# A gated mix of Fourier mixing and sliding-window attention: four engines in listed order, row sums inverted as 128 x 16, and earlier loads

## The chip, the cores and the metric

The kernel runs on one core of one Trainium2 chip. The metric is device time in microseconds (us) of one execution, lower is better. A core has a matrix engine (PE, TensorE), a vector engine (DVE, VectorE), an activation engine (ACT, ScalarE), a general engine (POOL, GpSimd) and a queue that issues data transfers (SP, SyncE). ACT can issue transfers too. Each of them works through its own list of instructions in the order of that list, and waits at an instruction until what it needs is there. "The order" below is the order of these lists.

## The reference

There are 2048 rows of 512 numbers, x. One branch is a Fourier mixing layer, the other an attention layer with 32 heads of 16 columns in which each row sees itself and the 255 rows before it. A gate per row mixes them.

```python
a = einsum("bsd,ed->bse", x, dft_hid_re); b = einsum("bsd,ed->bse", x, dft_hid_im)
y = einsum("ts,bse->bte", dft_seq_re, a) - einsum("ts,bse->bte", dft_seq_im, b)
q, k, v = (x @ wqkv).reshape(B, S, 3, 32, 16).transpose(2, 0, 3, 1, 4)
scores = einsum("bhqd,bhkd->bhqk", q, k) * 16 ** -0.5      # kept where 0 <= q - k < 256
o = einsum("bhqk,bhkd->bhqd", softmax(scores), v) @ wo     # heads joined
g = sigmoid((x * gate_w).sum(-1))
return g * y + (1 - g) * o
```

## The kernel before

**The dense part** is everything that is an ordinary matrix product: the projections of x to q and k (`dqk`, four groups of heads times four quarters of 512 rows), to v (`dv`, 16 blocks of 128 rows), to the two hidden Fourier products (`dab`), and the two sequence products with the 2048 x 2048 cosine and sine matrices (`dc`). It is written as a Python generator, `dense()`, which yields after every matmul, so that the attention loop can draw from it a few matmuls at a time. Each operand is split into a rounded part `hi` and a rest `lo`, and a product is three matmuls. While attention runs, a matmul is done as two halves of 64 rows of the contraction (L248, "64*128 64x512"), the upper half some time behind the lower one; a copy of one number by ACT (`token`, L267) stands between them. What follows a finished block (`then`, `late`) is listed when its upper half has been listed.

**The attention part** walks through 128 units n (8 sets of four heads times 16 blocks of 128 rows) with two pairs of heads p each. A step (n, p) lists, on PE, two score matmuls `s` (L396) on which DVE takes a masked row minimum of the negated scores (L400, written to `ml`), then dense matmuls (`fill`), then, 11 units later (`LAG`), the transposed scores `t` (L455), of which ACT takes the exponent (L458) into `pt` and POOL cuts the corners (L461, L465), then dense matmuls again. `FILL_PAIR` / 4 dense matmuls go into each `fill`; there are four per unit. `s` and `t` share four banks of PSUM, so an `s` may start only when DVE has read the one that had its bank. Every four units (one group u, 32 groups in all) the minima are turned with PE (L414), stored and loaded back as rows of the operand `ring` (`ml_split`, `ml_turn`, `ml_rows`, `m_ring`).

Every four units `visit` multiplies `pt` with v into one PSUM bank `o` (L482). v has a column of ones, so row 16 of every 32 rows of `o` holds the sums of the softmax. `o_take` (L495) then copies `o` with ACT into an `ev` buffer (L501), takes the reciprocal of the whole 128 x 512 bank with DVE into a second one (L502), and stores the four rows that matter to `l_scr` in DRAM with four transfers from SP. `o_load` (L507) loads each of them back to 32 partitions, and `o_out` (L512) multiplies (L516) and stores the result to `o_scr`. These three stand in the list `later`, with a due time in steps: 2n+1, 2n+3 and 2n+5, where a step is one (n, p) and the visit itself stands in step 2n+1. `ev` has five buffers, which hold the partial results of the dense part too.

**What sets the order.** PE works in the order in which the code lists its instructions (`manual_schedule` at L1008). ACT, DVE and SP do so only for the first instructions (L144); after that, and on POOL from the start, a scheduler of the framework orders them by its own estimate of time. Where the code says `behind("dve", "act")`, an instruction is held behind the last one marked on these engines.

**Partial results.** A block of `dc` is summed in two or four parts of 24 matmuls. `add_r` (L757) loads what was stored earlier from `r_scr` into an `ev` buffer and adds the new part to it on DVE (L763). `c_blocks` (L558) runs three blocks side by side.

**The start.** `qk_first` and the v blocks 0 to 3 (quarter 0) are listed before the loop (`need(("v", 3))`, L1012); quarters 1 to 3 are drawn in by `fill`. `ring_ahead` (L987) lists the loads of a quarter of `ring` as soon as its projection is in the stream, and forces the projection when the loop needs it. Attention takes 32 such quarter loads of eight transfers.

**The end.** After the loop `attention_done` (L850) switches the dense matmuls to full 128 rows; the rest of `dense()` follows, with the product with `wo` in eight pieces (`wo_begin` and its like, L929) between.

## Time and profile before

| what | value |
|---|---|
| time, median of 2 runs | 1011.27 us (1008.42 to 1014.12) |
| the profiled execution's own time | 1017.02 us |
| its span, first to last instruction | 1015.3 us |
| PE / DVE / ACT / POOL busy | 907.0 / 646.9 / 405.1 / 236.3 us |
| mean granted PE clock | 0.947 of full speed |
| transfers | 167.10 MB, 165 GB/s on average |

A profile page gives for each engine its busy time, a strip of 40 slices with the busy share in tenths, the clock that the throttle granted to PE, the queues, the chain of work that ended last, and the costliest groups of instructions. A group's row reads: line, engine, operation, output <- inputs, shapes, count; then busy us and mean ns of one; then the time for which the engine stood idle just before such an instruction, and what ended that. The view of waits adds these up by engine and releaser ("us in total, times, longest"). A row of the view in order of time gives start, duration, the instruction, and in brackets the idle time before it. "SPq" and "ACTq" are transfers being issued by SP and ACT. Busy time on PE is modelled from pipelined matmuls and is not the same as full use.

### The profile page before, as it was taken

What the parts mean: (1) busy time and instruction counts of PE and PEld (TensorE: products, weight loads), DVE (VectorE), ACT (ScalarE), POOL (GpSimd) and SP (SyncE); (2) the same over time, 40 slices, a digit from 0 to 9 for tenths busy, and PEclk for the clock granted to TensorE, in tenths of its full rate; (3) what the DMA queues carried; (4) which work ended last, traced back from release to release, by engine and by line L of the source; (5) the groups of instructions that cost most, each with busy time, mean ns of one, the idle gap of its engine ahead of it and who ended that gap; (6) DMA issues with size and microseconds to landing.
All of it is one profiled execution on the core that took longest, in us unless ns stands there. A gap on an engine that the chain in (4) does not pass through costs nothing. (4 is left out here: it accounts for less than half of the span.)

```text
span 1015.3 us, 21619 instructions
## 1 busy us (share of the span) xinstructions
PE 907.0 (89%) x7659; PEld 759.9 (75%) x7659; DVE 646.9 (64%) x1639; ACT 405.1 (40%) x1000; POOL 236.3 (23%) x529
## 2 busy tenths in 40 slices
PE   9785797899998998999998898879979989988898
PEld 8675675787776777888887787767767777776897
DVE  4553274576666766757766576567757767655884
ACT  4312352344452444444444444423334424652330
POOL 7001121122221222222222222212212212431440
PEclk9888798899998998999999999989989989999999
DMA  8759456566776635445564358867944442444833
GB/s 261 204 127 175 124 155 194 187 202 188 207 204 172 192 86 158 122 142 122 143 134 142 110 152 207 234 186 207 267 142 128 148 132 71 153 139 153 295 116 104
DMA packets 100908, 167.10 MB, mean 165 GB/s; under 512 B 29504, under 2 KB 39232, under 8 KB 100800
## 3 DMA queue, kind: packets, MB, share of 16 engines
q1 hardware_dynamic: 100368, 165.07, 57.4%
q8 instruction: 60, 0.98, 0.4%
q10 hardware_dynamic: 432, 0.66, 0.2%
q14 instruction: 48, 0.39, 0.1%
HBM read 113.25 MB, written 52.43 MB: 163 GB/s over the span
## 5 line engine op out<-in xcount | busy, mean ns | idle before, releaser
L248 PE MATMUL dc<-big,hi 64*128 64x512 f32 x1826 | 389.2, 404 | 0.4 <-ACT token L267 0.3
L400 DVE CUSTOM_DVE_ANT_0 junk<-s,mask 128x384 bf16<-128x384 f32 (+2 forms) x512 | 270.1, 528 | 156.0 <-PE s L396 103.0
L248 PE MATMUL dc<-big,lo 64*128 64x512 f32 x912 | 340.5, 405 | 3.6 <-DVE lo L607 3.6
L248 PEld LDWEIGHTS dc<-big,hi 64*128 64x128 f32 x1826 | 277.5, 192 | 6.5 <-ACT token L267 1.6
L458 ACT ACTIVATE pt<-t 128x384 f32<-128x384 f32 (+2 forms) x400 | 164.6, 475 | 164.1 <-PE t L455 129.7
L461 POOL TENSOR_SCALAR_AFFINE_SELECT pt<-pt 128x256 f32<-128x256 f32 x200 | 85.0, 425 | 558.4 <-ACT pt L458 519.2
L396 PE MATMUL s<-ring,ring 48*128 48x384 f32 (+2 forms) x512 | 152.5, 377 | 62.8 <-DVE ml L400 45.0
L248 PEld LDWEIGHTS dc<-big,lo 64*128 64x128 f32 x912 | 174.9, 192 | 6.1 <-DVE lo L607 4.0
L396 PEld LDWEIGHTS s<-ring,ring 48*128 48x128 f32 x512 | 92.6, 195 | 105.8 <-DVE ml L400 76.3
L502 DVE RECIPROCAL ev<-o 128x512 f32<-128x512 f32 x32 | 107.4, 3357 | 44.0 <-ACT ev L501 43.6
L455 PE MATMUL t<-ring,ring 50*128 50x384 f32 (+2 forms) x512 | 114.8, 352 | 9.5 <-DVE ml L400 9.2
L248 PE MATMUL dab<-hi,big 64*128 64x512 f32 x512 | 117.5, 412 | 0.1
L248 PE MATMUL dqk<-big,hi 64*128 64x512 f32 x480 | 116.8, 412 | 0.2
L607 DVE TENSOR_TENSOR lo<-raw,hi 128x512 fp32r<-128x512 f32 x142 | 98.7, 702 | 1.2 <-ACT hi L607 1.2
L607 ACT CAST hi<-raw 128x512 fp32r<-128x512 f32 x142 | 82.4, 623 | 39.4 <-PE dc L248 31.9
L248 PE MATMUL dab<-lo,big 64*128 64x512 f32 x256 | 96.5, 410 | 0.0
L455 PEld LDWEIGHTS t<-ring,ring 50*128 50x128 f32 x512 | 71.9, 188 | 31.3 <-DVE ml L400 17.2
L248 PE MATMUL dqk<-big,lo 64*128 64x512 f32 x240 | 92.5, 413 | 0.0
L248 PEld LDWEIGHTS dab<-hi,big 64*128 64x128 f32 x512 | 80.4, 195 | 4.3 <-DVE big L92 0.8
L248 PEld LDWEIGHTS dqk<-big,hi 64*128 64x128 f32 x480 | 77.8, 197 | 4.0 <-ACT token L267 0.9
L248 PE MATMUL dv<-hi,big 64*128 64x512 f32 x256 | 65.5, 415 | 13.3 <-ACT vst L352 13.3
L465 POOL TENSOR_SCALAR_AFFINE_SELECT pt<-pt 128x256 f32<-128x256 f32 x176 | 74.8, 425 | 0.0
(116 smaller groups left out, 1100.5 us busy)
## 6 DMA issues: line engine op xcount, KB each, us to landing
qk_scr<-home SPq DMA_DIRECT2D x64, 256.0 KB
ring<-qk_scr SPq DMA_DIRECT2D x128, 128.0 KB
raw<-cr SPq DMA_DIRECT2D x32, 512.0 KB
raw<-ci SPq DMA_DIRECT2D x32, 512.0 KB
r_scr<-ev SPq DMA_DIRECT2D x44, 256.0 KB
ab_scr<-home SPq DMA_DIRECT2D x20, 512.0 KB
big<-ab_scr SPq DMA_DIRECT2D x20, 512.0 KB
ring<-qk_scr SPq DMA_DIRECT2D x128, 64.0 KB
```

What stands on the lines that cost most here:

```text
L248: nc.tensor.matmul(ps, lhsT[r], rhs[r], start=start, stop=stop, tile_position=(64 * i, 0), skip_group_check=True)
L396: nc.tensor.matmul(pss[h][:, :w], ring[0][r, pair, j * BQ:(j + 1) * BQ], ring[1][r, pair, k0:k0 + w], start=True, stop=True, tile_position ...
L400: mark("dve", nc.vector.tensor_tensor_reduce(out=junk[:, :w], in0=pss[h][:, :w], in1=mask[:, WIN - w:], scale=1.0, scalar=3e38, op0=OP.add ...
L455: nc.tensor.matmul(pss[h][:, :w], ring[1][r, pair, q0:q0 + BQ], ring[0][r, pair, q0:q0 + w], start=True, stop=True, tile_position=(64 * h, 0))
L458: mark("t", nc.scalar.activation(pt[:, 2 * p + h, :w], pss[h][:, :w], AF.Exp, scale=-1.0))
L461: nc.gpsimd.affine_select(a, a, pattern=[[0, 2], [1, 128]], compare_op=OP.is_ge, fill=0.0, base=0, channel_multiplier=-1)
L465: nc.gpsimd.affine_select(a, a, pattern=[[0, 2], [-1, 128]], compare_op=OP.is_gt, fill=0.0, base=0, channel_multiplier=1)
L502: mark("dve", nc.vector.reciprocal(l, ps))
L607: return fn(*args)
```

## The change

Six things change.

- **Order.** ACT, DVE, SP and now POOL work in the order in which the code lists them from the first instruction until `attention_done`; there the manual order ends for them, and PE alone keeps it. `behind` does nothing until then.
- **Row sums.** `o_take` now only copies `o` with ACT; ACT itself issues the four stores of the raw sums. The 4 x 512 sums are then loaded back from `l_scr` as 128 partitions of 16 (`o_sums`), inverted by DVE in that shape and stored again (`o_turn`), and loaded to 32 partitions each (`o_load`) as before. The due times are 2n+2, 2n+4, 2n+6, 2n+7 and 2n+9.
- **Partial results ahead.** In the blocks of three of the second half, the load for `add_r` becomes a job listed early in the last part of the block instead of after it.
- **Start.** The loop begins after the q and k projection of the second quarter (`need(("qk", 0, 1))`).
- **Fill.** `FILL_PAIR` is 16.5 instead of 16.8.
- `full`, the list of finished groups, goes; the group's number is passed on.

```diff
--- before.py
+++ after.py
@@ -29,7 +29,7 @@
 WARM = 10
 BEHIND = 5
 SWITCH = 7
-FILL_FIRST, FILL_PAIR, FILL_T = 12, 16.8, 12
+FILL_FIRST, FILL_PAIR, FILL_T = 12, 16.5, 12
 
 
 @with_exitstack
@@ -63,6 +63,7 @@
 
 
     last = {}
+    free = []
 
     def mark(e, ins):
         last[e] = ins.ins
@@ -71,7 +72,7 @@
     def behind(*engines):
         with ExitStack() as es:
             for e in engines:
-                if e in last:
+                if free and e in last:
                     es.enter_context(tc.issue_after(last[e]))
             yield
 
@@ -141,7 +142,10 @@
     def pt_raw():
         return at.tile([P, 4, WIN], F32, name="pt", bufs=4).rearrange("p a b -> p (a b)")[:, :1024]
 
-    with tc.manual_schedule(engines={mybir.EngineType.Activation, mybir.EngineType.DVE, mybir.EngineType.SP}):
+    in_order = ExitStack()
+    in_order.enter_context(tc.manual_schedule(engines={mybir.EngineType.Activation, mybir.EngineType.DVE,
+                                                       mybir.EngineType.SP, mybir.EngineType.Pool}))
+    if True:
         wraw, *xraw = [pt_raw() for _ in range(3)]
         wq0 = [st.tile([P, 1024], F32R, name=h) for h in ("hi", "lo")]
         for dk in range(DK):
@@ -486,28 +490,30 @@
                                  skip_group_check=True)
             if e >= min(kb * BQ + WIN, S):
                 del PT[n]
-        if hi % 4 == 0:
-            full.append(lo // 4)
-
-    full = []
     OS = {}
 
-    def o_take():
-        u = full.pop(0)
+    def o_take(u):
         o = ev.tile([P, 512], F32, name="ev")
         l = ev.tile([P, 512], F32, name="ev")
-        ps = OT.pop()
-        with behind("dve", "act"):
-            mark("act", nc.scalar.copy(o, ps))
-            mark("dve", nc.vector.reciprocal(l, ps))
+        mark("act", nc.scalar.copy(o, OT.pop()))
         for t in range(4):
-            ld(l_scr[u][t:t + 1], l[32 * t + 16:32 * t + 17])
+            nc.scalar.dma_start(l_scr[u][t:t + 1], o[32 * t + 16:32 * t + 17])
         OS[u] = o, l
+
+    def l_rows(u):
+        return l_scr[u].rearrange("t (a b) -> (t a) b", b=16)
+
+    def o_sums(u):
+        ld(OS[u][1][:, :16], l_rows(u))
+
+    def o_turn(u):
+        l = OS[u][1][:, :16]
+        mark("dve", nc.vector.reciprocal(l, l))
+        ld(l_rows(u), l)
 
     def o_load(u):
         ls = l_scr[u]
-        with behind("sp"):
-            ld(OS[u][1], bass.AP(tensor=ls.tensor, offset=ls.offset, ap=[[512, 4], [0, 32], [1, 512]]))
+        ld(OS[u][1], bass.AP(tensor=ls.tensor, offset=ls.offset, ap=[[512, 4], [0, 32], [1, 512]]))
 
     def o_out(u):
         G, sb = divmod(u, 4)
@@ -555,13 +561,15 @@
                 if i != chunks[-1] or a == 0:
                     yield
 
-    def c_blocks(get, half, tbs, ab, done):
+    def c_blocks(get, half, tbs, ab, done, ahead=None):
         pss = {}
         for j in range(2):
             for tb in tbs:
                 w = get((half, tb * 2 + j))
                 if j == 0:
                     pss[tb] = ps_d.tile([P, 512], F32, name="dc", tag="d")
+                if j and ahead:
+                    jobs.append(lambda tb=tb: ahead(tb))
                 yield from c_part(w, range(16)[8 * j:8 * j + 8], ab, pss[tb], (0, 15))
                 if j:
                     then(lambda tb=tb: late(done, tb, pss[tb]))
@@ -754,12 +762,19 @@
         def r_in(tb):
             return r_scr[2 if tb in lasts else 0][tb]
 
+        ahead = {}
+
+        def load_r(tb):
+            ahead[tb] = ev.tile([P, 512], F32, name="ev")
+            ld(ahead[tb], r_in(tb))
+
         def add_r(tb, ps):
             r = mixed.pop(tb, None)
             late_r = r is not None
             if not late_r:
-                r = ev.tile([P, 512], F32, name="ev")
-                ld(r, r_in(tb))
+                if tb not in ahead:
+                    load_r(tb)
+                r = ahead.pop(tb)
             nc.vector.scalar_tensor_tensor(r, ps, g1[:, tb:tb + 1], r, op0=OP.mult, op1=OP.add)
             ld(out[tb] if late_r else r_scr[1][tb], r)
             if not late_r:
@@ -771,7 +786,7 @@
                                   add(lambda t: r_scr[2][t], lambda t: r_scr[1][t], wait.append),
                                   None if j else next_b)
         for three in threes[1]:
-            yield from c_blocks(pieces.get, 1, three, ab, add_r)
+            yield from c_blocks(pieces.get, 1, three, ab, add_r, load_r)
         assert Halves.whole
         for tb in (13, 14):
             yield from c_blocks(pieces.get, 1, (tb,), ab, add_r)
@@ -849,6 +864,10 @@
 
     def attention_done():
         all_rows()
+        in_order.close()
+        free.append(True)
+        last.clear()
+        ctx.enter_context(tc.manual_schedule(engines={mybir.EngineType.PE}))
         RT.append(const.tile([P, 6, 512], F32, name="rt", tag="home"))
         new = const.tile([P, NB * 4 * HV + 16], F32, name="oraw", tag="vall"), \
             at.tile([P, 4, WIN], F32, name="pt", bufs=4).rearrange("p a b -> p (a b)")
@@ -1005,11 +1024,11 @@
             next(stream, None)
             quota -= 1
 
-    ctx.enter_context(tc.manual_schedule(engines={mybir.EngineType.PE}))
+    in_order.enter_context(tc.manual_schedule(engines={mybir.EngineType.PE}))
     TURN = (4, 0, ml_split), (4, 1, ml_turn), (5, 0, ml_rows), (7, 0, m_ring)
     need(("qk", 0, 0))
     ring_ahead(0)
-    need(("v", 3))
+    need(("qk", 0, 1))
 
     summed = 0
     later = []
@@ -1050,7 +1069,9 @@
                     if G < 2 * NG - 1:
                         for c in [sb - 1] * (sb > 0) + [3] * (sb == 3):
                             v_load(4 * (G + 1) + c)
-                    later += [(2 * n + 1, o_take), (2 * n + 3, lambda u=u: o_load(u)), (2 * n + 5, lambda u=u: o_out(u))]
+                    later += [(2 * n + at, lambda do=do, u=u: do(u)) for at, do in
+                              ((2, o_take), (4, o_sums), (6, o_turn), (7, o_load), (9, o_out))]
+                    later.sort(key=lambda x: x[0])
                 if k < NU:
                     t_pair(k, 0)
             if 0 <= k < NU and (p or not due):
```

The first place is SP, around the group u = 12 in the middle of the program (`l_scr_181` is its store; `rows` are minima, `o_scr` results of the group before, `raw` a piece of the cosine matrix). Before:

```order
L59 DMA raw<-cr 128x1024
L59 DMA r_scr_1_206<-ev 128x512
L59 DMA l_scr_181<-ev 1x512 x4
L59 DMA raw<-cr 128x1024
L59 DMA ev<-l_scr_181 128x1x512
L59 DMA m_scr_152<-rows 32x128
L59 DMA r_scr_2_207<-ev 128x512
L59 DMA o_scr_201<-ev 16x512 x4
L59 DMA raw<-cr 128x1024
```

and now:

```order
L59 DMA o_scr_204<-ev 16x512 x4
L59 DMA raw<-cr 128x1024
L59 DMA r_scr_2_207<-ev 128x512
L59 DMA m_scr_152<-rows 32x128
L59 DMA ev<-l_scr_181 128x16
L59 DMA raw<-cr 128x1024
L59 DMA l_scr_181<-ev 128x16
L59 DMA ev<-l_scr_181 128x1x512
L59 DMA ring_287<-qk_scr_2_1_90 32x2x512
L59 DMA ring_288<-qk_scr_2_1_106 16x2x512
```

The four stores of the sums have left SP; in their place stand a load as 128 x 16, a store as 128 x 16 and the broadcast load, behind which eight loads of `ring` now come at once.

The second place is DVE in the same group, at the reciprocal. Before (`o` is the PSUM bank):

```order
L400 ISA ml 128x1
L502 RECIPROCAL ev<-o 128x512
L407 CAST mhl<-ml 128x16
L607 TENSOR_TENSOR lo<-raw,hi 128x512
L400 ISA junk,ml<-s,mask 128x128
```

and now (L511 is the reciprocal, L404 the row minimum, L615 a split of `raw`):

```order
L404 ISA junk,ml<-s,mask 128x384
L404 ISA ml 128x1
L615 TENSOR_TENSOR lo<-raw,hi 128x512
L511 RECIPROCAL ev<-ev 128x16
L404 ISA junk,ml<-s,mask 128x384
```

The reciprocal stands between row minima as before, on 16 columns instead of 512, and reads a buffer that a transfer has filled.

The third place is ACT in the same group, at the copy of `o`. Before:

```order
L607 CAST hi<-raw 128x512 x2
L458 ACTIVATE pt<-t 128x384 x2
L501 COPY ev<-o 128x512
L458 ACTIVATE pt<-t 128x384 x4
L267 COPY token<-dc 1x1
```

and now (L462 is the exponent, L498 the copy):

```order
L615 CAST hi<-raw 128x512
L462 ACTIVATE pt<-t 128x384 x2
L498 COPY ev<-o 128x512
L500 DMA l_scr_181<-ev 1x512 x4
L271 COPY token<-dc 1x1
L462 ACTIVATE pt<-t 128x384 x2
```

Four transfers now stand behind the copy in ACT's list, ahead of the next exponents.

The fourth place is PE at the first scores. Before, they stand among the projections of the second quarter:

```order
L248 MATMUL dv<-lo,big 128x512
L248 MATMUL dqk<-big,hi 128x512
L248 MATMUL dv<-hi,big 128x512
L396 MATMUL s<-ring_289,ring_288 128x128 x2
L248 MATMUL dqk<-big,hi 128x512 x2
L248 MATMUL dqk<-big,lo 128x512
```

and now behind them, with the v block that follows:

```order
L252 MATMUL dqk<-big,hi 128x512
L252 MATMUL dv<-hi,big 128x512
L252 MATMUL dqk<-big,lo 128x512
L400 MATMUL s<-ring_288,ring_287 128x128 x2
L252 MATMUL dv<-lo,big 128x512
L252 MATMUL dv<-hi,big 128x512 x2
```

The first scores have moved behind the 24 matmuls of `dqk` of the second quarter.

## The prediction

> **What bounds the kernel now.** The page first. PE is the busiest engine, and its clock was not granted in full everywhere.
>
> ```profile
> span 1015.3 us, 21619 instructions
> ...
> PE 907.0 (89%) x7659; PEld 759.9 (75%) x7659; DVE 646.9 (64%) x1639; ACT 405.1 (40%) x1000; POOL 236.3 (23%) x529
> ...
> PEclk9888798899998998999999999989989989999999
> ```
>
> PE is idle for 1015.3 - 907.0 = 108 us. Next the stretches: the start with the first scores (25 to 125 us), the long attention stretch (to 895 us), and the end.
>
> ```profile
> 25.00:125.00 100.00, 72.58 (x573) 64.03 (x569) 45.09 (x156) 25.57 (x64) 6.12 (x16) 0.83 0.66 161
> 125.00:895.00 770.00, 702.99 (x6248) 581.58 (x6240) 510.87 (x1329) 331.46 (x832) 180.60 (x452) 0.96 0.58 163
> 895.00:1015.00 120.00, 108.12 (x735) 93.68 (x727) 79.25 (x135) 36.26 (x81) 31.64 (x40) 0.95 0.49 159
> ```
>
> The fourth number is PE busy, the one before the DMA share the clock. PE loses 27 us in the first stretch, 67 in the second, 12 in the last. The clock takes 0.17 x 100 = 17 us more in the first and 0.04 x 770 = 31 us in the second. Then the waits of PE, asked for the first two stretches apart (total, times, longest):
>
> ```profile
> PE s L396 <- DMA ring<-qk_scr: 13.6, 6, 5.1
> PE dv L248 <- ACT vst L352: 13.3, 1, 13.3
> ...
> PE s L396 <- DVE ml L400: 44.5, 58, 6.0
> PE t L455 <- DVE ml L400: 9.2, 14, 2.0
> PE s L414 <- DVE ml L400: 4.1, 7, 1.8
> PE s L414 <- DVE mhl L408: 3.5, 2, 2.1
> ```
>
> In attention 44.5 + 9.2 + 4.1 + 3.5 = 61.3 of PE's 67 idle us end with DVE, although DVE is busy for only 511 of 770 us. So DVE is late at places, not short of time. The groups say where:
>
> ```profile
> L502 DVE RECIPROCAL ev<-o 128x512 f32<-128x512 f32 x32 | 107.4, 3357 | 44.0 <-ACT ev L501 43.6
> L516 DVE TENSOR_TENSOR ev<-ev 128x512 f32<-128x512 f32 x32 | 22.7, 709 | 77.1 <-DMA ev<-l_scr 73.1 <-issue 3.9
> L224 DVE RECIPROCAL g<-ge 128x16 f32<-128x16 f32 x1 | 0.3, 254 | 0.0
> ```
>
> Once per group of four units DVE spends 3.36 us on a reciprocal, 1.4 us before it waiting for the copy, and 73.1 / 32 = 2.3 us before the multiplication waiting for the broadcast of the sums. I went through PE's 81 waits for DVE in this stretch one by one: 42 begin within 5 us after a reciprocal's end (24.8 us in all), 28 within 5 us after the start of a multiplication (28.6 us), 11 after neither (7.8 us). First and last of the first two kinds, and the largest with its cause:
>
> ```profile
> 132.39 0.29 PE L414 MATMUL s<-ident,mhl 64*128 64x64 f32 x1 [0.15 <-DVE ml L400]
> 845.11 0.44 PE L396 MATMUL s<-ring,ring 48*128 48x384 f32 x1 [0.27 <-DVE ml L400]
> 142.89 0.43 PE L396 MATMUL s<-ring,ring 48*128 48x384 f32 x1 [0.53 <-DVE ml L400]
> 855.51 0.44 PE L396 MATMUL s<-ring,ring 48*128 48x384 f32 x1 [0.18 <-DVE ml L400]
> 173.29 0.69 DVE L516 TENSOR_TENSOR ev<-ev 128x512 f32<-128x512 f32 x1 [7.61 <-DMA ev<-l_scr]
> 174.52 1.40 PE L396 MATMUL s<-ring,ring 48*128 48x384 f32 x2 [6.04 <-DVE ml L400]
> ```
>
> DVE stood for 7.61 us, PE for 6.04: the banks of `s` and `t` cover the first 1.6 us or so, the rest goes through.
>
> **The clock** costs on top of each gap:
>
> ```profile
> 449.29 0.65 PE L414 MATMUL s<-ident,mhl 64*128 64x64 f32 x2 [1.36 <-DVE mhl L408]
> ...
> 448.00:450.00 2.00, 0.65 (x6) 0.54 (x8) 1.94 (x9) 0.00 (x0) 0.40 (x2) 1.00 0.01 4
> 450.00:452.00 2.00, 2.00 (x15) 1.61 (x14) 1.23 (x7) 0.87 (x3) 0.00 (x0) 0.69 0.43 82
> 452.00:454.00 2.00, 2.00 (x12) 2.00 (x11) 0.37 (x2) 1.77 (x4) 0.68 (x2) 0.50 0.57 221
> ```
>
> After a gap of 1.36 us the clock is 0.69 and 0.50 in the next two slices, which is (0.31 + 0.50) x 2 = 1.6 us lost. I therefore count the clock's 31 us as following the gaps in proportion. [...]
>
> **The change part by part**, against the profiled execution (1017.0 us, of which 1015.3 span).
>
> *Reciprocal.* L224 is a reciprocal of the new shape: 254 ns. DVE is relieved of 32 x (3.357 - 0.254) = 99 us, and of the wait for the copy in front. The 24.8 us of PE behind reciprocals go, but the small one now stands behind a load and can itself be late. What that load costs no row shows: from -24.8 (never late) to 0 (late as often as now). I take -22, since two steps lie between load and use; the next rows say what that is worth.
>
> *The chain of the sums.* Transfers and use now, in a quiet and in a busy group, in time order by queue and engine:
>
> ```profile
> 448.11 1.13 SPq L59 DMA_DIRECT2D l_scr<-ev  x4
> 450.76 0.53 SPq L59 DMA_DIRECT2D ev<-l_scr  x1
> 457.25 0.69 DVE L516 TENSOR_TENSOR ev<-ev 128x512 f32<-128x512 f32 x1 [2.00 <-DMA ev<-l_scr]
> 457.97 1.69 SPq L59 DMA_DIRECT2D o_scr<-ev  x4
> ...
> 161.52 2.21 SPq L59 DMA_DIRECT2D l_scr<-ev  x4
> 166.99 0.56 SPq L59 DMA_DIRECT2D ev<-l_scr  x1
> ```
>
> A small store takes 2.7 us to be readable when it is quiet, 5.5 when it is busy; the broadcast takes 457.25 - 450.76 = 6.5 us. A group lasts 770 / 32 = about 24 us, a step 3 us. Now the broadcast has two steps, 6 us for 6.5: it is just late, as the 2.0 us show. After the change the chain has two transfers more (the sums back, the inverse out). Each of the first hops has two steps (6 us for 2.7 to 5.5). The inverse store has one step (3 us) before SP, in order, waits for it at the broadcast's load; the broadcast has two steps, of which the second holds the visit, so rather 8 us. In a quiet group nothing is late; in a busy one SP starts the broadcast some 2.5 us late, and DVE waits about 1 us. Bounds: -28.6 (never late) to +28.6 (the waits double). I take half, -14.
>
> *Order.* SP issues 64 transfers fewer, and the queues carry nearly the same bytes. In listed order each DVE or ACT instruction waits at most for something listed before it, and PE is in the same list already, so I price it at nothing where the chain above doesn't hold it. POOL's order is nearly the same, and it is busy for 23%.
>
> *ACT* now issues four transfers per group.
>
> ```profile
> L150 ACTq DMA_DIRECT2D pt<-xT x2: 413/433/453, 0.8 to 1.2; - x2
> ...
> ACT ev L501 <- PE o L482: 75.2, 24, 5.5
> PE s L396 <- ACT pt L458: 1.9, 5, 0.8
> ```
>
> At 0.433 us that is 1.7 us per group, 55 us of ACT in all; from 0 (hidden) to 55 (none hidden). The nearest row decides: today ACT stands for 75.2 / 24 = 3.1 us at the copy, at the same place, and PE waited for its exponents for 1.9 us in all. One step later that wait is over by itself, and 1.7 us take its place. I take +4.
>
> *Start.* 24 `dqk` matmuls move ahead of the first scores, so the ring load of a quarter is listed two units before its use instead of in the unit before.
>
> ```profile
> 46.03 0.66 PE L396 MATMUL s<-ring,ring 48*128 48x384 f32 x1 [5.07 <-DMA ring<-qk_scr]
> ...
> 79.48 22.55 SPq L59 DMA_DIRECT2D ring<-qk_scr  x40
> ```
>
> Two units are 24 matmuls and their scores, some 6 us, against a longest wait of 5.07: of the 13.6 us I take -12, and of the clock's 17 us -8 (bounds 0 and -25 together). The 13.3 us for `vst` stay: the 40 ring loads still stand in one piece in SP's list, ahead of the v store that PE waits for.
>
> *Clock in attention.* 36 of 67 idle us go, so 31 x 36 / 67 = -17.
>
> *Fill, and loads ahead.* 0.3 x 117 units = 35 matmuls leave the loop, 24 enter before it: 11 more at the end.
>
> ```profile
> 508.88 0.39 PE L248 MATMUL dc<-big,lo 64*128 64x512 f32 x1
> 509.89 0.39 PE L248 MATMUL dc<-big,lo 64*128 64x512 f32 x1
> ```
>
> Nine halves start between these two, so a whole matmul takes 1.01 / 4.5 = 0.22 us; 2.5 us move to the end and as much leaves the loop. The loads for `add_r` only start earlier and hold one `ev` buffer longer: nothing, unless an `ev` copy then waits. The last group's longer chain at the end I put at +2, a small store from the rows above.
>
> Sum: -22 - 14 + 4 - 12 - 8 - 17 + 2 = -67, so 950 in the profile. The median of the runs shown lies 5.8 us below the profiled execution: **945 us**, and I round the doubt about new waits up to 950.
>
> **Rivals.** *The chain takes the place of the reciprocal.* If every hop takes the busy time, DVE is late at the small reciprocal and at the multiplication: +28.6 instead of -14, no clock back in attention, -22 and the start's -20 remain: 1011 - 22 + 29 - 20 + 4 = 1002, no change. For it: two more transfers, and DMA shares of 0.58. Against: the due times lie one to four steps later. [...]
>
> *ACT is held by its own transfers* (slower). In the built program each transfer also waits for an earlier one that used the same of eight completion counters, and that is often one of the `o_scr` stores listed one step before, which follow the multiplication (457.97 after 457.25). If the broadcast is late, so are they, and ACT stands with the next exponents behind it. It decides from the point where ACT stands longer than the 3.1 us that are hidden now. With 2 us over that in each of 31 groups and 1.6 us of clock: 31 x 3.6 = 112 us, on top of -67: 1011 + 45 = 1056.
>
> [...]
>
> *Everything smooth.* All 61.3, all 13.6 and all clock after them (31 + 10): 1011 - 116 = 895.
>
> That the order doesn't change is excluded by the rows on SP, which differ from the first group on.
>
> **How the numbers follow.** Forecast (930 to 980) 0.52, clock rule 0.08, smooth 0.10; the chain instead of the reciprocal 0.17; ACT held 0.13. Faster by over 2% (below 991): 0.70; within 2%, about what a measurement of this kernel can tell from no change: 0.17; slower: 0.13. The range leaves out ACT held and the far end of smooth: 910 to 1003.
>
> **What would show it.** The reciprocal's group at about 0.25 us x32; PE's wait for DVE in attention below 30 us; no ring wait over 2 us before 125 us, but `vst` still about 13; a mean clock of 0.96 or more. ACT's wait before exponents with PE waiting on ACT for more than 10 us would show the second rival, an idle time of over 100 us before reciprocal and multiplication together the first. The forecast is wrong if a hop of the chain takes longer than its steps, since then DVE stands as it does now.

## The result, and the profile after

The changed kernel takes 1083.05 us (1081.87 to 1084.24, 2 runs) against 1011.27: a ratio of 1.071, 95% interval 1.0571 to 1.0849. It is slower, and the forecast of 950 with its range of 910 to 1003 was wrong. The head of the profile after, in the order of the head of before (span, busy times, granted clock in 40 slices):

```profile
span 1080.1 us, 21572 instructions
...
PE 926.9 (86%) x7648; PEld 783.7 (73%) x7648; DVE 557.2 (52%) x1639; ACT 403.3 (37%) x999; POOL 239.2 (22%) x529
...
PEclk9996978988788989898989998889789999997999
```

DVE has 90 us less to do, as it was to be. PE is busy 20 us longer, though it runs 11 instructions fewer, and idle for 153 us instead of 108. 20 + 45 are the 65 us between the spans. The stretches of start, attention and end (PE busy is the fourth number, the clock stands ahead of the DMA share):

```profile
25.00:125.00 100.00, 74.80 (x647) 66.52 (x644) 49.20 (x170) 31.25 (x78) 8.37 (x22) 0.90 0.67 171
125.00:945.00 820.00, 708.00 (x6047) 592.34 (x6049) 421.12 (x1313) 320.45 (x808) 180.87 (x440) 0.89 0.53 151
945.00:1080.00 135.00, 119.97 (x813) 102.83 (x809) 75.83 (x137) 39.62 (x91) 32.06 (x46) 0.94 0.47 149
```

In the start the clock rose as forecast (0.83 to 0.90). Most of the loss is in attention: from the first scores to the last it takes 876 us now and took 832 before, and in the long stretch PE is idle for 112 us at a clock of 0.89 (67 at 0.96 before). By the mean granted clock, 0.902 now and 0.947 before, the share of the clock that was not granted is (1 - 0.902) x 1080 = 106 us of the span, against 54 before; below this is called slow clock. PE's waits in attention, from 125 to 815 us, a window that lies inside attention in every kernel below:

```profile
PE s L400 <- DVE ml L404: 29.9, 29, 4.1
PE s L400 <- ACT pt L462: 29.5, 12, 5.2
PE s L400 <- ACT home L462: 20.0, 4, 7.8
PE dc L252 <- ACT token L271: 13.4, 3, 7.2
PE dqk L252 <- ACT token L271: 6.3, 3, 3.6
PE dab L252 <- ACT token L271: 3.9, 2, 2.6
```

What ended with DVE has fallen from 56 to 31 us. But 73 us end with ACT, where before there were 2. ACT is busy for only 403 us, so it is held; its own waits say by what:

```profile
ACT pt L462 <- DMA l_scr<-ev: 49.8, 8, 9.7
ACT token L271 <- DMA l_scr<-ev: 44.1, 8, 8.9
...
ACT home L462 <- DMA l_scr<-ev: 19.0, 2, 9.9
```

These are exponents and tokens that stood behind the four stores of the raw sums which ACT now issues: 113 us in 18 waits, 6.3 us a time. And the new chain of the sums, by groups (multiplication, copy, small reciprocal):

```profile
L522 DVE TENSOR_TENSOR ev<-ev 128x512 f32<-128x512 f32 x32 | 23.5, 736 | 114.5 <-DMA ev<-l_scr 60.0 <-DMA ring<-qk_scr 47.5 <-issue 7.0
...
L498 ACT COPY ev<-o 128x512 f32<-128x512 f32 x32 | 19.1, 596 | 3.5 <-PE o L486 3.5
...
L511 DVE RECIPROCAL ev<-ev 128x16 f32<-128x16 f32 x32 | 7.8, 245 | 4.6 <-DMA ev<-l_scr 4.6
```

The reciprocal takes 0.245 us instead of 3.357. The multiplication's idle time grew from 77 to 114 us.

**One group, close up.** In order of time: the transfers that SP issues, ACT, then PE (around 434 us):

```profile
431.08 2.84 SPq L59 DMA_DIRECT2D big<-ab_scr  x4
433.97 0.59 SPq L59 DMA_DIRECT2D ring<-m_scr  x2
...
435.71 4.17 SPq L59 DMA_DIRECT2D o_scr<-ev  x4
```

```profile
432.12 0.60 ACT L498 COPY ev<-o 128x512 f32<-128x512 f32 x1
439.76 1.96 ACTq L500 DMA_DIRECT2D l_scr<-ev  x4
441.77 0.87 ACT L462 ACTIVATE home<-t 128x384 f32<-128x384 f32 x2 [9.05 <-DMA l_scr<-ev]
```

```profile
442.31 1.07 PE L400 MATMUL s<-ring,ring 48*128 48x384 f32 x2 [7.79 <-ACT home L462]
```

The copy ends at 432.7, but the first of ACT's stores goes out only at 439.8. In the built program the four wait for the completion of earlier transfers, all SP's:

```
l_scr, 1st row  waits for  ring<-m_scr   (SP)
l_scr, 2nd row  waits for  ring<-m_scr   (SP)
l_scr, 3rd row  waits for  vall<-v_scr   (SP)
l_scr, 4th row  waits for  raw<-cr       (SP)
```

Every transfer of the built program waits like this: the transfers take eight completion counters in turn, and each waits for the one before it on its counter, that is for the one listed eight transfers earlier (1076 of 1084 here and 1012 of 1020 in the kernel before; the first eight have none). No store to `o_scr` is among the four. `ring<-m_scr` is small, but four large loads were issued just ahead of it. Sizes of one transfer in this window, by the view of the transfers:

```profile
big<-ab_scr SPq DMA_DIRECT2D x4, 512.0 KB
...
l_scr<-ev ACTq DMA_DIRECT2D x4, 2.0 KB
ring<-m_scr SPq DMA_DIRECT2D x2, 8.0 KB
```

The windows of 2 us show the pile being moved (the last number is GB/s) and PE with nothing to do:

```profile
434.00:436.00 2.00, 0.53 (x7) 0.29 (x3) 0.01 (x1) 0.00 (x0) 0.00 (x0) 1.00 1.02 389
436.00:438.00 2.00, 0.00 (x0) 0.00 (x0) 0.00 (x0) 0.00 (x0) 0.00 (x0) 0.69 0.89 334
438.00:440.00 2.00, 0.00 (x0) 0.00 (x0) 0.00 (x0) 0.00 (x0) 0.00 (x0) 0.50 1.06 367
440.00:442.00 2.00, 0.00 (x0) 0.00 (x0) 0.00 (x0) 0.23 (x1) 0.00 (x0) 0.50 0.24 83
442.00:444.00 2.00, 1.69 (x7) 1.59 (x9) 0.82 (x2) 1.15 (x3) 0.77 (x2) 0.50 0.00 1
```

ACT's stores leave as the pile runs out. Its 8 KB of sums stood behind 2 MB of the Fourier branch, and the exponents, PE and the clock (still 0.50 in the slice in which PE is back) behind the sums.

The other groups differ in which transfer it is. Of the 128 stores, 49 wait in the built program for a store to `o_scr` and 79 for something else. In the trace ACT stands for 129 us ahead of these stores in all 32 groups (gaps over 0.3 us, issuing not counted); 8 of these us lie ahead of a store that waits for `o_scr`.

### The profile page after: what moved, and what is told of

Its sections match the earlier page's. It is cut to its first block, busy times and chain, and to the rows that moved or that the text cites. A ratio compares the mean times of both kernels' runs of the same rounds, so it can differ in the third digit from the quotient of the medians.

```text
span 1080.1 us, 21572 instructions
## 1 busy us (share of the span) xinstructions
PE 926.9 (86%) x7648; PEld 783.7 (73%) x7648; DVE 557.2 (52%) x1639; ACT 403.3 (37%) x999; POOL 239.2 (22%) x529
## 4 chain that ended last, share of the span: by engine, by line
PE 48%; DMA 33%; DVE 5%; issue 4%; ACT 4%; SPq 3%; ACTq 2%; DVEq 0%
PE dc L252 18%; DMA ring<-qk_scr 11%; DMA ev<-l_scr 7%; PE dab L252 6%; PE dqk L252 6%; PE s L400 4%; PE o L486 4%; PE dc L264 4%; PE t L959 3%; SPq L59 3%; DMA l_scr<-ev 3%; DVE junk L404 3%; DMA vall<-v_scr 2%; PE dv L252 2%; PE t L459 2%
## 5 line engine op out<-in xcount | busy, mean ns | idle before, releaser
L252 PE MATMUL dc<-big,hi 64*128 64x512 f32 x1812 | 400.1, 417 | 26.5 <-ACT token L271 19.7
L404 DVE CUSTOM_DVE_ANT_0 junk<-s,mask 128x384 bf16<-128x384 f32 (+2 forms) x512 | 270.5, 528 | 207.8 <-PE s L400 122.2
L252 PE MATMUL dc<-big,lo 64*128 64x512 f32 x904 | 348.5, 418 | 0.0
L252 PEld LDWEIGHTS dc<-big,hi 64*128 64x128 f32 x1812 | 287.3, 200 | 40.0 <-ACT token L271 24.3
L462 ACT ACTIVATE pt<-t 128x384 f32<-128x384 f32 (+2 forms) x400 | 163.6, 473 | 243.0 <-PE t L459 153.4
L465 POOL TENSOR_SCALAR_AFFINE_SELECT pt<-pt 128x256 f32<-128x256 f32 x200 | 86.3, 431 | 605.5 <-ACT pt L462 433.7
L252 PE MATMUL dab<-hi,big 64*128 64x512 f32 x512 | 125.3, 438 | 3.9 <-ACT token L271 3.9
L615 DVE TENSOR_TENSOR lo<-raw,hi 128x512 fp32r<-128x512 f32 x142 | 100.9, 714 | 47.3 <-ACT hi L615 47.2
L459 PE MATMUL t<-ring,ring 50*128 50x384 f32 (+2 forms) x512 | 121.6, 364 | 3.0 <-DVE ml L404 1.8
L252 PE MATMUL dab<-lo,big 64*128 64x512 f32 x256 | 106.2, 444 | 0.0
L615 ACT CAST hi<-raw 128x512 fp32r<-128x512 f32 x142 | 86.7, 623 | 39.1 <-DMA l_scr<-ev 12.6
L252 PEld LDWEIGHTS dab<-hi,big 64*128 64x128 f32 x512 | 87.4, 212 | 8.1 <-ACT token L271 5.7
L522 DVE TENSOR_TENSOR ev<-ev 128x512 f32<-128x512 f32 x32 | 23.5, 736 | 114.5 <-DMA ev<-l_scr 60.0
L462 ACT ACTIVATE home<-t 128x384 f32<-128x384 f32 (+2 forms) x112 | 45.9, 468 | 87.0 <-PE t L459 52.6
```

What stands on the lines that cost most here:

```text
L252: nc.tensor.matmul(ps, lhsT[r], rhs[r], start=start, stop=stop, tile_position=(64 * i, 0), skip_group_check=True)
L404: mark("dve", nc.vector.tensor_tensor_reduce(out=junk[:, :w], in0=pss[h][:, :w], in1=mask[:, WIN - w:], scale=1.0, scalar=3e38, op0=OP.add ...
L459: nc.tensor.matmul(pss[h][:, :w], ring[1][r, pair, q0:q0 + BQ], ring[0][r, pair, q0:q0 + w], start=True, stop=True, tile_position=(64 * h, 0))
L462: mark("t", nc.scalar.activation(pt[:, 2 * p + h, :w], pss[h][:, :w], AF.Exp, scale=-1.0))
L465: nc.gpsimd.affine_select(a, a, pattern=[[0, 2], [1, 128]], compare_op=OP.is_ge, fill=0.0, base=0, channel_multiplier=-1)
L522: mark("dve", nc.vector.tensor_mul(o, o, l))
```

## The experiments

The theories at the outset: **T1**, ACT is held by its own transfers; **T2**, listed order costs by itself; **T3**, the chain of the sums is too long for its due times. Every ratio is to the kernel before, run with it on the same chip; 1% is about 10 us.

### Which part of the change costs

**e1**: the changed kernel, the stores back on SP.

```diff
-            nc.scalar.dma_start(l_scr[u][t:t + 1], o[32 * t + 16:32 * t + 17])
+            ld(l_scr[u][t:t + 1], o[32 * t + 16:32 * t + 17])
```

> The changed kernel, with the four small stores of the sums issued by SP again instead of ACT; all else as changed. T1 (ACT is held by its own transfers: 130 us of ACT's waits before 23 groups of exponents, 85 us of PE behind them, and the clock after those gaps): the waits go, 85 us and some 50 us of clock come back, 1083 becomes 940 to 990, and PE's wait for ACT in attention falls under 10 us. T2 (the listed order of the engines' queues costs by itself): the order is as before, so 1065 to 1090. T3 (the longer chain makes the multiplication late): DVE's 114 us of idle time before the multiplication stay or grow, the stores now also wait in SP's queue, 1040 to 1090.

**e2**: the kernel before, with listed order alone.

```diff
-    with tc.manual_schedule(engines={mybir.EngineType.Activation, mybir.EngineType.DVE, mybir.EngineType.SP}):
+    in_order = ExitStack()
+    in_order.enter_context(tc.manual_schedule(engines={mybir.EngineType.Activation, mybir.EngineType.DVE,
+                                                       mybir.EngineType.SP, mybir.EngineType.Pool}))
```

> The kernel before, with ACT, DVE, SP and GpSimd in listed order until attention ends; the old reciprocal, the old chain and the old start. T1: nothing holds ACT, so 995 to 1025, no change. T2: the listed order is what costs, 1060 or more, with waits of PE for ACT and DVE like those of the changed kernel. My prediction priced it at nothing: 1011.

**e3**: the kernel before, with the new functions of the sums alone, ACT's stores included.

```diff
-                    later += [(2 * n + 1, o_take), (2 * n + 3, lambda u=u: o_load(u)), (2 * n + 5, lambda u=u: o_out(u))]
+                    later += [(2 * n + at, lambda do=do, u=u: do(u)) for at, do in
+                              ((2, o_take), (4, o_sums), (6, o_turn), (7, o_load), (9, o_out))]
```

> The kernel before, its order still set by the scheduler, with the new way of the sums alone (copy, four stores by ACT, load of 128 rows of 16, small reciprocal, store, broadcast, multiplication a step or two later each). T1: ACT is held here as well, 1050 to 1100, with some 50 us or more of PE's waits ending with ACT. T2: without the listed order the new chain does what I predicted, 960 to 990. T3: 1000 to 1030, the wait of DVE in front of the multiplication grows beyond 100 us and takes back what the reciprocal gave.

**e4**: the kernel before, with the early start and its fill.

```diff
-    need(("v", 3))
+    need(("qk", 0, 1))
-FILL_FIRST, FILL_PAIR, FILL_T = 12, 16.8, 12
+FILL_FIRST, FILL_PAIR, FILL_T = 12, 16.5, 12
```

> The kernel before, with only the early start of the scores (behind the second quarter instead of the values) and the fill of 16.5. My prediction's terms for these: the 13.6 us of PE's waits for the ring go (-12) and some clock with them (-8), so 985 to 1000. Rival: the stall for the values' store takes back what the ring waits gave, since 24 matmuls moved ahead do not make the store any earlier (13.3 us before, 20.9 us in the changed kernel): 1005 to 1020.

**e16**: the kernel before, with the loads of the partial results a part ahead, alone.

```diff
+                if j and ahead:
+                    jobs.append(lambda tb=tb: ahead(tb))
```

> The kernel before, with only the loads of the partial results a part ahead. My prediction: nothing, so 1005 to 1025. Rival (the fifth ev buffer is missing to the copies): 1025 or more.

| part | time (us) | ratio, 95% interval |
|---|---|---|
| e2, listed order alone | 1063.11 | 1.0438 (1.0376 to 1.0500) |
| e3, new sums alone, stores by ACT | 1072.23 | 1.0546 (1.0491 to 1.0600) |
| e4, early start and fill alone | 994.75 | 0.9787 (0.9744 to 0.9829) |
| e16, loads ahead alone | 1016.45 | 0.9970 (0.9940 to 1.0001) |
| e1, all of the change, stores by SP | 1004.99 | 0.9863 (0.9786 to 0.9940) |

The four parts add up to +4.4 + 5.5 - 2.1 - 0.3 = +7.5%, and the whole is +7.1%. T1 holds: e1 moves one instruction's issuer and gives back 1.071 - 0.986 = 8.5%, and PE's waits for ACT in the window fall from 73 to 2 us. It ends at 1005, though, not below 990, so T1 is smaller than I had put it, and something else is left. In e3 as well ACT holds PE, with no listed order; the two largest of those waits:

```profile
PE t L455 <- ACT pt L458: 22.1, 7, 5.8
PE s L396 <- ACT pt L458: 17.3, 7, 11.9
```

T2 holds in e2, with a mechanism that I had not seen. First the largest of PE's waits in e2, then the group of its reciprocal:

```profile
PE t L459 <- DVE ml L404: 32.6, 43, 2.0
PE s L400 <- DVE ml L404: 20.5, 23, 3.0
```

```profile
L506 DVE RECIPROCAL ev<-o 128x512 f32<-128x512 f32 x32 | 107.4, 3356 | 92.6 <-ACT ev L505 87.8 <-ACT token L271 3.9 <-ACT token L288 0.8
```

In listed order DVE stands at the old reciprocal for ACT's copy, 92.6 us in place of 44.0, with the row minima behind it. The new way has no such pair side by side, since the small reciprocal comes two hops after the copy. e16 confirms the price of nothing.

### T3: the chain, and whether listed order costs with it

**e5**: the kernel before, with the new sums, stores by SP. **e6**: e5 with the early start of e4.

> The kernel before, its order still set by the scheduler, with the new way of the sums and its four stores issued by SP; no early start, no listed order. T1 (ACT's own transfers were the cost of the new way): against the same with ACT's stores (1072) the 66 us of PE's waits for ACT and their clock go, so 975 to 1000; the reciprocal's 22 us come back as predicted. T3 (two transfers more make the multiplication late, as with SP's stores in listed order, where DVE stood 142 us before it): 1000 to 1025, the reciprocal's gain is given back. T2: free order is better than listed order also with this chain, so below 1000 - 5 in any case when the early start is added.

> The same as e5 with the early start and the fill of 16.5, that is the changed kernel without listed order, without loads ahead and with SP's stores. If the parts add up: e5 less 22 us (995 against 1018 was the early start's). T2 (listed order costs 40 us with the new chain too): 945 to 970, against 1005 in listed order. Rival (listed order costs only with the old chain, where the copy and the long reciprocal are listed too early): 990 to 1010, the same as in listed order.

e5 took 1012.69 us, ratio 0.9964 (0.9934 to 0.9995); e6 1008.38, ratio 0.9898 (0.9833 to 0.9964). The new sums bring nearly nothing without ACT's part in them: the reciprocal's gain is given back. And e6 stands within 1% of e1 (1004.99, 0.9863), in which the order is listed: with this chain the order costs nothing. So the sum above fits by chance: e2's loss belongs to the old chain and is not in the changed kernel. What listed order seems to do there is to make ACT's hold dearer, 8.5% (e1) against 1.0546 - 0.9964 = 5.8% in the scheduler's order (e3 and e5); but e3 and e5 also lack the early start. The chain in e1, the multiplication and the small reciprocal:

```profile
L522 DVE TENSOR_TENSOR ev<-ev 128x512 f32<-128x512 f32 x32 | 23.5, 734 | 141.7 <-DMA ev<-l_scr 98.9 <-DMA ring<-qk_scr 36.3 <-DMA ev<-r_scr 6.5
...
L511 DVE RECIPROCAL ev<-ev 128x16 f32<-128x16 f32 x32 | 7.9, 248 | 39.7 <-DMA ev<-l_scr 39.6
```

**e8**: e1 with later due times; the sums get a small tile of their own, so that the broadcast's buffer is taken only at its load. **e11**: e1 with that tile and only the last hop later.

First the due times of e8, then those of e11:

```diff
-                              ((2, o_take), (4, o_sums), (6, o_turn), (7, o_load), (9, o_out))]
+                              ((2, o_take), (4, o_sums), (7, o_turn), (9, o_load), (12, o_out))]
```

```diff
-                              ((2, o_take), (4, o_sums), (6, o_turn), (7, o_load), (9, o_out))]
+                              ((2, o_take), (4, o_sums), (6, o_turn), (7, o_load), (12, o_out))]
```

> The changed kernel with SP's stores (1005) and later due times: sums back still at 4, the small reciprocal at 7 instead of 6, the broadcast's load at 9 instead of 7, the multiplication at 12 instead of 9; the small reciprocal works in a tile of its own, the broadcast's buffer is taken at its load. T3 (what is left of the loss is the chain that is shorter than its transfers: DVE stands 142 us before the multiplication and 40 us before the reciprocal): both fall below 40 us together, PE's wait for DVE from 56 to below 25, and the time to 955 to 985. Rival (the waits of DVE are hidden mostly, and the buffers now held longer stall ACT's copy or SP's loads): 1000 to 1020.

> SP's stores and only the last hop later: reciprocal at 6 and broadcast's load at 7 as in the changed kernel, the multiplication at 12 instead of 9 (the small reciprocal in a tile of its own). T3a (the broadcast's two steps were the step that was too short; DVE stood 142 us at the multiplication): 950 to 970, nearly all of the 49 us. T3b (SP is held by the inverse store that it must wait for, and DVE stood 40 us at the small reciprocal): 975 to 1000, at most half of it.

**e10**: e8 with the four small stores in one. **e12**: e8's chain and the early start, in the scheduler's order, without the loads ahead.

```diff
-        for t in range(4):
-            ld(l_scr[u][t:t + 1], o[32 * t + 16:32 * t + 17])
+        ld(l_scr[u], o[16::32])
```

> The version at 956 (SP's stores, later due times) with the four small stores made into one of four rows. SP issues 96 transfers fewer, and each of its transfers waits for one eight back: if SP's queue is still late at places, 940 to 955; if not, 950 to 962, no change.

> SP's stores, the later due times and the early start, but the order of ACT, DVE, SP and GpSimd set by the scheduler as in the kernel before; no loads ahead. Listed order cost 44 us with the old chain and nothing with the new one at its short due times (1008 and 1005). If it costs nothing with this chain either: 945 to 970. If the free order is better once the chain is no longer late: below 945. If the scheduler moves the pieces back together and undoes the later due times: 985 to 1010.

| kernel | time (us) | ratio, 95% interval | DVE idle at the reciprocal | at the multiplication |
|---|---|---|---|---|
| e1 | 1004.99 | 0.9863 (0.9786 to 0.9940) | 39.7 | 141.7 |
| e11, last hop later | 975.24 | 0.9593 (0.9528 to 0.9658) | 44.0 | 18.0 |
| e8, all later | 956.20 | 0.9394 (0.9341 to 0.9448) | 5.1 | 67.3 |
| e10, and one store | 954.96 | 0.9381 (0.9314 to 0.9448) | 7.7 | 70.8 |
| e12, later, scheduler's order | 942.83 | 0.9273 (0.9211 to 0.9334) | 13.1 | 57.1 |

T3 holds for the time of e8, but not for its signs: DVE still stands for 72 us at the two places, where I had expected less than 40, and PE's waits for DVE in the window are 38 us, not below 25. Later due times, with the small tile and no work taken away, are worth 4.7%. The last hop has 2.7% of it, so T3a has the larger part, but e11 stays outside its 950 to 970, just inside T3b's 975 to 1000, and the small reciprocal is as late as before. The number of SP's transfers is not the matter (e10). With this chain the scheduler's order is better by 1.2% (e12 beside e8; the loads ahead, which e12 lacks, are worth nothing by e16).

### T1: is ACT's hold a cost of its own?

**e7**: the changed kernel, ACT's four stores in one. **e9**: e8 with the four stores on ACT again.

```diff
-        for t in range(4):
-            nc.scalar.dma_start(l_scr[u][t:t + 1], o[32 * t + 16:32 * t + 17])
+        nc.scalar.dma_start(l_scr[u], o[16::32])
```

> The changed kernel with ACT's four small stores of the sums made into one store of the same four rows; still on ACT, listed order and all else as changed. T1 in the form 'each transfer waits for an earlier one that shares its completion counter': one wait instead of four, for the oldest of the eight transfers before, so ACT's 130 us of waits for transfers fall to under 40 and the time to 1000 to 1035. If instead the issuing itself, or the reading of the copy, held ACT, then a quarter to a half of the loss stays at best: 1045 to 1080.

> The changed kernel with the four stores still on ACT, but with the later due times (7, 9, 12) that brought the version with SP's stores from 1005 to 956. T1 (ACT's hold and the late chain are two costs): the 50 us of the chain come back, ACT's waits stay, so 1010 to 1050 with over 40 us of PE's waits ending with ACT. Rival (ACT is held only because the chain is late and drags the earlier transfers with it, so the due times were the one cause): 955 to 985.

e7 took 1029.53 us, ratio 1.0106 (1.0038 to 1.0173): of the 8.5% that e1 gives back, 6.0% are back with three stores fewer. In the built program each group's store now waits for one earlier transfer in place of four. Most of ACT's hold is still there, though. From the end of the copy to the end of the last store's issue 4.5 us pass per group in the window, issuing included, 112 us in 25 groups, against 6.3 us, 146 in 23, in the changed kernel; I had expected less than 40 in all. (The view of waits has 72 against 152 us, but it puts part of e7's down to PE.) So 1.8 us less per group gave back most of the loss: PE's waits for ACT fell from 73 to 42 us, and the clock in the window rose from 0.88 to 0.94.

e9 took 1002.86, ratio 0.9836 (0.9750 to 0.9923): 4.4% above e8, a little less than my 1010 to 1050. ACT holds PE for 57 us in the window, and DVE is no longer late:

```profile
PE s L400 <- ACT pt L462: 32.3, 13, 10.3
PE s L400 <- ACT home L462: 11.0, 5, 5.0
```

```profile
L523 DVE TENSOR_TENSOR ev<-ev 128x512 f32<-128x512 f32 x32 | 21.8, 682 | 15.4 <-DMA ev<-l_scr 13.5 <-DMA raw<-cr 1.4 <-DMA qk_scr<-home 0.5
```

So the hold does not follow from the late chain alone.

### Why the chain is long

Still open was why a broadcast that I gave two steps, "6 us for 6.5", was late by so much. e13 changes no due time, only the form of that load: four loads, each of one row of sums into 32 partitions, instead of one load from four rows.

```diff
-        ld(OS[u][1], bass.AP(tensor=ls.tensor, offset=ls.offset, ap=[[512, 4], [0, 32], [1, 512]]))
+        for t in range(4):
+            ld(OS[u][1][32 * t:32 * t + 32], bass.AP(tensor=ls.tensor, offset=ls.offset + 512 * t, ap=[[0, 32], [1, 512]]))
```

**e13**: e1 with this. **e15**: the kernel before with this. **e14**: e12 with this. **e17**: the changed kernel with this, ACT's stores kept.

> The version with SP's stores at the short due times (1005), with the broadcast's load split in four, one row of sums each into 32 rows; nothing is listed later. T3c (the hop is long by the transfer's form: 7 to 8.5 us from issue to use, one load from four rows): DVE's 142 us of idle time before the multiplication fall below 70, and the time to 965 to 985. Rival (the hop is long because the queue around it is full): three more transfers per group, 1000 to 1015. [...]

> The kernel before, with only the broadcast's load in four. T3c: of the 77 us of idle time before the multiplication most go, and the 28.6 us that PE waits behind multiplications with them, and some clock: 975 to 1000. Rival: 1010 to 1025.

> The best version so far (943: SP's stores, later due times, early start, the scheduler's order) with the broadcast's load in four. T3c: 57 us of DVE's idle time before the multiplication are left there, with some 27 us of PE behind DVE; half of that comes back: 925 to 940. Rival: 943 to 955.

> The changed kernel itself (1083), with only the broadcast's load split in four. T1 (ACT's hold is a cost of its own: 78 us at short due times, 47 at the later ones): the 61 us that the split gave with SP's stores come back, the hold stays, so 1000 to 1030, with over 40 us of PE's waits ending with ACT. Rival (ACT is held only because the broadcast is late and with it the output stores that ACT's transfers wait for): 940 to 965.

| kernel | without: us, ratio | with: us, ratio and 95% interval |
|---|---|---|
| changed, stores by SP (e1, e13) | 1004.99, 0.9863 | 943.98, 0.9281 (0.9256 to 0.9306) |
| before (e15) | 1 | 985.09, 0.9676 (0.9646 to 0.9706) |
| later due times, scheduler's order (e12, e14) | 942.83, 0.9273 | 925.17, 0.9083 (0.9043 to 0.9123) |
| changed, stores by ACT (e17) | 1083.05, 1.071 | 1028.85, 1.0095 (1.0048 to 1.0141) |

The broadcast's issue and the multiplication that waits for it, in e1 and then in e13:

```profile
502.14 0.54 SPq L59 DMA_DIRECT2D ev<-l_scr  x1
...
510.69 0.69 DVE L522 TENSOR_TENSOR ev<-ev 128x512 f32<-128x512 f32 x1 [3.64 <-DMA ev<-l_scr]
```

```profile
514.20 1.71 SPq L59 DMA_DIRECT2D ev<-l_scr  x4
...
518.60 0.69 DVE L523 TENSOR_TENSOR ev<-ev 128x512 f32<-128x512 f32 x1 [1.30 <-DMA ev<-l_scr]
```

and the multiplication's group in e13:

```profile
L523 DVE TENSOR_TENSOR ev<-ev 128x512 f32<-128x512 f32 x32 | 22.4, 701 | 47.2 <-DMA ev<-l_scr 40.3 <-DMA ring<-m_scr 6.9
```

The same 256 KB take 8.6 us from issue to use as one load and 4.4 us as four. Over all groups in which the multiplication waits for this load, the median is 7.2 us in e1 (22 groups, 5.2 to 9.0) and 3.9 us in e13 (19 groups, 3.4 to 7.7). T3c holds, and in e13 by more than I had put on it: 5.8%, where I had expected 965 to 985 us. In the kernel before it is worth 3.2%, though 39.5 of the 77 us before the multiplication stay. e13 at the changed kernel's short due times is as fast as e12 at the later ones. The DMA share differs as the durations do, first in the kernel before at the end of the quiet group's broadcast, with hardly anything else under way, then in e13 while the four loads run:

```profile
456.00:456.50 0.50, 0.50 (x8) 0.50 (x6) 0.00 (x0) 0.00 (x0) 0.50 (x2) 1.00 0.25 95
```

```profile
515.00:516.00 1.00, 1.00 (x13) 1.00 (x11) 0.89 (x3) 0.12 (x1) 0.00 (x0) 1.00 0.48 131
```

The one load kept the 16 engines busy for a quarter of the time (0.25, at 95 GB/s); with the four under way it was 0.48, at 131 GB/s, with whatever else ran counted in. How either form is spread over the engines was not shown. Whether four pieces of another form would do as well was not tried.

e17 settles what ACT's stores are: with a broadcast that is quick the changed kernel is still 8.1% above e13. In the window 79 us of PE's waits end with ACT, and 6 with DVE. The largest of each in e17:

```profile
PE s L400 <- ACT pt L462: 37.0, 12, 9.7
...
PE s L400 <- DVE ml L404: 5.3, 15, 1.9
```

The version e14, at 925 us, is faster than both kernels: ratio 0.9083 to before.

## Why the prediction was wrong

The forecast was 950 us and the result 1083. About 80 us of that are ACT's part (e1), and most of the rest is the chain's: e13, without ACT's hold and with the quick broadcast, takes 944 us. That this is close to the forecast is luck, since its hop is shorter than the one that I had priced.

**ACT: the step that failed.** I put the four transfers at "+4", between 0 and 55, from the row of their issue (0.433 us each) and from the 3.1 us for which ACT stood at the copy, hidden, before. Measured, they cost 8.5% (e1), 8.1% (e17) or 4.4% (e9), some 45 to 85 us. What the row of issues can't show is the wait in front, for other transfers to complete; it averages 6.3 us where it shows. My second rival named that wait, with 2 us over the hidden 3.1 and a chance of 0.13, and its sign that PE would wait for ACT for more than 10 us came true with 73. It tied the wait to the `o_scr` stores behind a late broadcast, though. e17 and e9 cut that tie, and so does the trace: only 8 of ACT's 129 us lie ahead of a store that waits for `o_scr`. The close-up shows another cause, four loads of 512 KB ahead of the small transfers. That the 3.1 us did not hide it I can only argue: they were spent waiting for PE's `o`, while PE had its own work. Whether the same stores would cost less behind the next exponents in ACT's list was not tried.

**The chain.** "-14", "two steps, of which the second holds the visit, so rather 8 us": wrong in sign. With the stores on SP the multiplication's idle time went from 77 to 142 us, and 40 us in front of the reciprocal came on top. The first rival's 1002 describes e1 (1005) and e6 (1008) to 1%. The 6.5 us that I took for the broadcast were not far off: where the multiplication waits for it, the median is 6.4 us in the kernel before and 6.9 in the changed one. What failed is the length of the steps. Behind the small reciprocal I allowed one step of 3 us and two of 8 together; in the changed kernel DVE comes to the multiplication 6.5 us after the reciprocal, while the inverse store takes 2.9 us until SP sends the broadcast and the broadcast another 7.2 until its use (medians of groups 5 to 28). So the multiplication is some 3.5 us late in a usual group, not about 1 in a busy one. Nor did I ask why the broadcast took so long. The due times that the chain needs are nearer to e8's; better still is the shorter hop of e13. Whether the rows of 64 B cost anything was not tried apart.

**Order.** "At nothing": wrong for the kernel before (e2, +4.4%), where the wait for ACT's copy ahead of the row minima doubled; right for the new chain (e6 beside e1); and wrong by 1.2% where the chain has room (e12 beside e8). That each instruction waits only for what is listed earlier excludes a deadlock, not a loss.

**Reciprocal.** Its duration was right (0.245 for 0.254 us), and in the changed kernel it stood late for 4.6 us in all (in e1 for 39.7). Its -22 can't be seen alone: in e5 reciprocal and chain together come to -0.4%.

**Start and fill.** -20 forecast, -2.1% measured (e4), about 22 us: right in size, but partly by luck. In e4 the ring waits of 13.6 us before 125 us are gone but for 0.2, as they are in the changed kernel. The stall for `vst`, which I left at 13.3, grew to 20.5 us, however, so that PE's idle time in this stretch falls by only 6 us and slow clock by 5. Another 8 us or so are less slow clock in attention, which I had not put down to the start. The same stall in the changed kernel:

```profile
PE dv L252 <- ACT vst L356: 20.9, 1, 20.9
```

Beside a late chain the same edit gave only 0.7% (e6 beside e5).

**Clock.** The -17 hung on idle time that was to go; it grew, and slow clock with it, from 54 to 106 us. That slow clock costs PE such sums is borne out in part: in e14 PE is busy 861 us for the same work, 46 less than before, and at a mean clock of 0.968 slow clock takes 30 us there, 24 less. What the other 22 are stays open.

```profile
PE 861.2 (93%) x7648; PEld 740.7 (80%) x7648; DVE 555.2 (60%) x1639; ACT 407.2 (44%) x999; POOL 240.3 (26%) x529
```

**Loads ahead.** Nothing, as forecast (e16).

## What to carry to other kernels

A transfer's issue time is not the price of issuing it from a compute engine: read what the transfer must wait for before it can leave, and which large transfers stand ahead of that, because everything behind it on that engine waits too (here exponents and tokens for 113 us in the window, and PE for 73 us behind ACT). A load that copies few source rows many times may be slow by its form (here 7.2 us as one load, 3.9 in four); look at its time from issue to use, and try it in several pieces before moving due times. And when an edit lengthens a chain of transfers, compare each hop over many groups with the time after which the engine really comes to the use, not with a planned number of steps, before crediting what the edit takes away.

## What the runs showed of the hardware

One load of 256 KB from four rows, 32 copies each, took 7.2 us from issue to use (median of 22 groups, e1) where four loads of 64 KB took 3.9 (19 groups, e13); that one line of access pattern was worth 3.2% in the kernel before and 5.8% in e13.

The clock falls without long gaps. From 125 to 825 us PE is idle for 66 us in e2 and 61 in the kernel before. The longest gap is 3.0 us in e2 and 6.0 before. Gaps over 3 us are one in e2 and three before; gaps of 1 to 3 us are 25 in e2, 41 us together, and 13 before, 21 us together. The granted clock of e2 is the lower one:

```profile
125.00:825.00 700.00, 633.71 (x5401) 521.75 (x5399) 444.09 (x1177) 286.00 (x710) 152.67 (x385) 0.93 0.58 161
```

```profile
125.00:825.00 700.00, 638.51 (x5657) 528.20 (x5647) 466.01 (x1233) 297.72 (x744) 159.05 (x403) 0.96 0.60 167
```

(e2 first, then the kernel before.) In the traces' records of the clock the slow stretches in this window are at half clock and last 3.4, 6.8 or 10.2 us, 23 in e2 and 11 before; in the 3.4 us ahead of each PE stood for 1.0 to 2.7 us. So the run with fewer gaps over 3 us, and more of 1 to 3 us, has the lower clock (0.93 against 0.96). Which property of the gaps decides stays open: no run varied it alone.
